# A recurrence and eight hashed experts on one core: the first decay products turned in SBUF, slot tables built by matrix products, experts with 416 places

## The chip, the core and the metric

The kernel runs on one core of a Trainium2 chip. It is one launch that computes two blocks one after the other: an RWKV-7 recurrence, and a layer of eight experts whose tokens are chosen by a hash. The metric is the device time in microseconds (us). It was measured in three runs of the kernel before, and one further execution was taken with the hardware profiler. All times below are in us unless marked ns.

## The reference, cut to what matters

```python
# block 1: B=4, H=8, S=768, D=40, float32
for t in range(S):
    y[:, :, t] = einsum('bhd,bhde->bhe', r_t, state)
    Sa = einsum('bhde,bhe->bhd', state, a_t)
    state = state * w_t[:, :, None, :] - outer(Sa, b_t) + outer(v_t, k_t)
# bridge: (B,H,S,D) -> x of shape (B*S, H*D) = (3072, 320)
# block 2: E=8 experts, F=1024
expert_idx = token_ids * 2654435761 % 8
for e in range(E):
    mask = expert_idx == e
    out[mask] = maximum(x[mask] @ w1[e], 0) @ w2[e]
```

The multiplier of the hash is 1 modulo 8, so the expert of a token is given by the low three bits of its id. For the inputs that `setup_inputs()` makes, the eight experts get 387, 359, 415, 376, 364, 403, 371 and 397 tokens.

## The kernel before, in words

**Block 1.** The sequence is cut into 12 chunks of 64 steps. A tile `u` (0 to 23) is one chunk for two of the four batches, with 128 partitions (2 batches x 64 steps). The state update inside a chunk is rewritten with running products of the decays `w`. They are formed by `decays` (L305) in six rounds. A round covers two chunks for all 32 pairs of batch and head; its 128 partitions are four half chunks of 32 steps x 32 pairs, and a partition holds 32 steps x 40 values. VectorE multiplies forwards into `pb` (L336) and backwards into `qb` (L341), joins the segments (`own` L348 and L351, `ends`, `rends` L362 to L366), and scales both arrays (L372, L379). A later step needs them the other way round, with the time step on the partition. For that, `store` (L317) writes both to DRAM as rows `p_rows` and `q_rows` (eight DMAs of 160 KB, in pieces of 40 values, which are 160 bytes), and `tile_a` loads the rows of its tile from there into `pl` and `ql` (L420, L421, by GpSimd's queue). The loads of `a`, `b`, `k`, `r` and `v` (helper `load`, L297, SyncE's queue) also move 160-byte pieces, 512 of them in each DMA.

For each tile, `tile_a` forms `at` and `z` on VectorE (L431, L435), has them transposed by TensorE (`z_ps` L449, `t_ps` L486), and multiplies them (`a_ps`). `group_i` (L498) inverts the triangular blocks of four tiles at once, in 60 small VectorE steps (L527, L534) between transposes on VectorE (L509, L542, L543). `tile_m`, `tile_s` and `tile_b` carry the state through the chunk on TensorE, eight tiles behind `tile_a`; `tile_b` ends with the product `y_ps` and writes the rows of `x` to DRAM (L697).

**Order.** Every step is entered in a list with a time in ticks (`at_tick`), one tick per tile. The list is sorted and issued in that order, so TensorE, VectorE, ScalarE and GpSimd each take their instructions in the order of the ticks. SyncE's DMA queue is not under this list; the framework's scheduler orders it. Each queue is served in order: a DMA that waits for its data holds back those behind it. The product `y_ps` of tile `u` has the tick `u + 9` (and a part of one for its place in the chunk).

**Routing.** `routing()` is a generator whose pieces are put at ticks by the loop at its end. It ranks each token within its expert (eight instructions or so at a time, all on 128 x 24 or 128 x 192 values). From the rank it makes the token's slot. Each expert has 448 slots: three full tiles of 128 and a half tile of 64. The inverse table, from slot to token, is made by 24 indirect DMAs on GpSimd's queue that write 4-byte token numbers to `slot_tokens` in DRAM (L815), and ten loads of it into `idx_all` (L823, L827).

**Block 2.** For each expert the rows of `x` are gathered by `idx_all` (L886), transposed (`xg_ps` L895) and placed as columns `xt` (128 x 3 x 448). `up` (L912, L917) makes `ht` (eight blocks of 128 features x 448 tokens, each in a PSUM bank), and VectorE and ScalarE apply the maximum. `down` (L930) multiplies 128 tokens by `w2` and scatters the rows to the output (L935). A matrix product in float32 is recorded as two MATMUL instructions. The half tiles of two experts share one output tile: two chains of products with 64 tokens each fill the lower and the upper 64 partitions of one PSUM tile, in turn.

Tokens beyond the slots of an expert, or decays outside of limits, are handled by loops that are entered only if there are any; they run no pass on these inputs.

Of the kernel before, what the change touches and what calls it, by code (L numbers as in the profile page):

```python
# [42 lines left out]
def kernel(  # L44
# [13 lines left out]
    nc = tc.nc  # L58
# [14 lines left out]
    SLOTS = 448  # L73
    TPE = SLOTS // P
    SZ = 64
    UPE = SLOTS // SZ
    NST = E * UPE
    NOV = (N - SLOTS) // SZ
    NT = NST + NOV
    assert UPE == 2 * TPE + 1  # L80
# [24 lines left out]
    WP = 4  # L105
# [21 lines left out]
    def early_weights():  # L127

        t1 = [early.tile([P, F], F32, tag=n, name=f"w1_0{n}")[:] for n in ("pk", "nb", "ub")]
        t1[2] = t1[2][:, 0:FH]  # L130
        w1s[0] = t1
# [173 lines left out]
    def decays(ri, t_w, t0, span, t_f, span_f, stores=None):  # L305
# [8 lines left out]
        def store(i, src):  # L314
            dma = nc.scalar.dma_start if ri == 0 and i == 0 else nc.sync.dma_start
            for y in range(2 * RN):
                dma(pq_dram[ri][i][y * HC:(y + 1) * HC].rearrange("t bh e -> bh t e"),  # L317
                                  src[y * BH:(y + 1) * BH].rearrange("p (t e) -> p t e", e=D))

# [24 lines left out]
        def _():  # L344
# [3 lines left out]
            nc.scalar.copy(own[:, SEG - 1], q[:, SEG - 1, 0])  # L348
# [19 lines left out]
        @then.append  # L368
        def _():

            p = segs(x["pb"])
            nc.vector.tensor_tensor(p, p, x["rends"][:].unsqueeze(2).to_broadcast([P, SEG, SL, D]), op=OP.mult)  # L372
            if stores is None:
                store(0, x["pb"])

        @then.append
        def _():
# [3 lines left out]
            nc.scalar.copy(x["qb"][:, HC * D:], x["ends"][:, SEG])  # L381
            if stores is None:
# [17 lines left out]
        for i, f in enumerate(then):  # L400
            at_tick(t_f + span_f * i / len(then), order=8)(f)
# [4 lines left out]
    def tile_a(u):  # L406
# [6 lines left out]
        def _():  # L413
# [4 lines left out]
            p_rows, q_rows = (d[rn * C:(rn + 1) * C] for d in pq_dram[ri])  # L418
            for be in range(2):
                nc.gpsimd.dma_start(pl[half(be)], of_batches(p_rows, 2 * g + be, 1))  # L420
                nc.gpsimd.dma_start(ql[half(be)], of_batches(q_rows, 2 * g, 2))  # L421
# [5 lines left out]
        @at_tick(u - 0.6)  # L427
# [10 lines left out]
        @at_tick(u, "at_t")  # L438
# [4 lines left out]
        @at_tick(u, "z")  # L443
# [9 lines left out]
        @at_tick(u, "a")  # L453
# [41 lines left out]
    def group_i(gi, t0, t1, t2):  # L495
# [4 lines left out]
        def _():  # L500
            x["u"] = ub = early.tile([P, BLK * BLK], F32, tag="ub", name="ub")[:]
# [5 lines left out]
        def _():  # L507
            x["n"] = nb = early.tile([P, BLK * BLK], F32, tag="nb", name="nb")[:]
            nc.vector.transpose(paired(nb).rearrange("p s t k -> p t s k"), paired(x["pk"]).rearrange("p t h k -> p t k h"))  # L509
# [27 lines left out]
        def _():  # L537

            ub = paired(x["u"])
            x["ug"] = ug = work.tile([P, BLK * BLK], F32, tag="ug", name="ug", bufs=1)  # L540
            x["ut"] = ut = work.tile([P, BLK * BLK], F32, tag="ut", name="ut", bufs=1)
            nc.vector.transpose(paired(ut[:]).rearrange("p g s k -> p s g k"), ub.rearrange("p s t k -> p s k t"))  # L542
            nc.vector.transpose(paired(ug[:]).rearrange("p g t k -> p t g k"), ub.rearrange("p s t k -> p t s k"))  # L543

    def tile_m(u, t0):
# [6 lines left out]
        def _():  # L552
            ut, ug = (paired(groups[gi][n][:])[:, ti * H // 2:(ti + 1) * H // 2] for n in ("ut", "ug"))
# [159 lines left out]
    decays(0, -4.0, -3.0, 0.4, -2.5, 0.3)  # L713
    decays(1, -2.9, -1.9, 0.4, -1.4, 0.3, stores=0.36)
    decays(2, -0.65, 0.42, 0.8, 1.45, 0.6, stores=3.34)
    for ri in range(3, NR):
        t0 = ri * RN * NG - 5.0
        decays(ri, t0 - 1.0, t0, 0.7, t0 + 1.0, 0.3)
# [11 lines left out]

    idx_all = route.tile([P, E * TPE + E // 2], I32)
    src_all = route.tile([P, E * TPE + E // 2], I32)
    num = route.tile([1, NT], F32)
    owner = route.tile([1, NT], F32)

    def routing():
# [6 lines left out]
        token = const.tile([P, TPP], I32)  # L743
        nc.gpsimd.iota(token[:], pattern=[[1, TPP]], base=0, channel_multiplier=TPP)
# [385 lines left out]
```

## Time and profile before

| what | us |
|---|---|
| median of three runs (lowest to highest) | 724.65 (721.87 to 730.36) |
| the profiled execution | 728.74 |
| its span, first to last instruction | 727.0 |
| first `z_ps` product (tile 0) | starts at 33.8 |
| transposes that end the first group (`ut`, L542) | start at 119.4 |
| first `y_ps` with `mr` (tile 0, tick 9) | starts at 146.9 |
| last `y_ps` with `mr` (tile 23) | starts at 443.7 |
| first `up_ps` (expert 0) | starts at 458.8 |
| last output scatter (L935) | starts at 718.5 |

The profile gives for each engine the instructions with their lines. PE is TensorE's products, PEld its weight loads, DVE is VectorE, ACT is ScalarE, POOL is GpSimd, and a q behind an engine's name is its queue of DMA issues (SPq is SyncE's). TensorE is busy in 83% of the span, VectorE in 48%, and the mean granted TensorE clock is 0.923. The 16 DMA engines move 205,669 packets, of which 186,687 have less than 512 bytes. These shares are means over very different stages, so the reading below goes by stages.

### The profile page before, as it was taken

Reading aid. Unit: us, or ns where it says so; the run is one execution under the profiler, and the core shown is the slowest. Engines: PE = TensorE matmul, PEld = TensorE weight load, DVE = VectorE, ACT = ScalarE, POOL = GpSimd, SP = SyncE. Lnnn points to the kernel's source line nnn. Section 1 sums busy time; section 2 is a strip of 40 time slices with the busy share of each in tenths; the row PEclk is TensorE's granted clock in tenths of the full one; section 3 lists DMA queues with packets and bytes.
Section 4 is the critical chain, followed back from the end, with each engine's and each line's share of the span. In section 5 each row is a group of like instructions: output and inputs, shape, how many; then the busy total and the mean of one; then the engine's idle time right before and its main releaser. Section 6 shows DMA issues by size and latency. Waiting matters only on the chain.

```text
span 727.0 us, 21410 instructions
## 1 busy us (share of the span) xinstructions
PE 600.8 (83%) x9032; PEld 449.7 (62%) x9032; DVE 352.0 (48%) x879; ACT 297.3 (41%) x689; POOL 221.9 (31%) x360
## 2 busy tenths in 40 slices
PE   0146224899979998999999993999999999999994
PEld 0135223787868887888988983465655656565652
DVE  7685556897588797579498221222020202112010
ACT  4135312676637676777766661012131313101010
POOL 0415564233325323524232222512213031212101
PEclk9976565999979999999999998799999999999998
DMA  8999968987786668785334414924262553223000
GB/s 158 163 175 152 110 75 112 147 150 130 126 176 143 113 129 145 154 160 127 60 84 90 89 39 119 262 82 129 80 207 63 145 198 138 50 94 101 27 11 20
DMA packets 205669, 86.07 MB, mean 118 GB/s; under 512 B 186687, under 2 KB 196160, under 8 KB 205569
## 3 DMA queue, kind: packets, MB, share of 16 engines
q1 hardware_dynamic: 189056, 46.29, 37.0%
q0 software_dynamic: 12160, 37.06, 19.2%
q10 hardware_dynamic: 4352, 1.31, 0.9%
q8 instruction: 72, 1.18, 0.7%
q14 instruction: 29, 0.23, 0.1%
HBM read 68.85 MB, written 16.42 MB: 117 GB/s over the span
## 4 chain that ended last, share of the span: by engine, by line
PE 45%; issue 21%; DVE 11%; DMA 9%; SPq 6%; POOL 4%; ACT 3%; POOLq 0%; DVEq 0%; ACTq 0%
PE up_ps L912 6%; PE dn_ps L930 6%; PE y_ps L278 5%; PE rc_ps L278 4%; PE s_ps L278 3%; PE r_ps L278 3%; SPq L297 3%; SPq L317 3%; DMA qb<-in_w_dram 3%; PE x_t_ps L645 3%; PE t_ps L486 2%; POOL out_dram L935 2%; PE z_ps L449 2%; DMA kb<-in_k_dram 2%; PE nc_ps L278 2%
## 5 line engine op out<-in xcount | busy, mean ns | idle before, releaser
L920 DVE TENSOR_SCALAR ht<-up_ps 128x448 f32<-128x448 f32 x32 | 20.0, 625 | 195.6 <-PE up_ps L917 129.7
L930 PE MATMUL dn_ps<-w,ht 128*128 128x320 f32 (+1 forms) x448 | 109.5, 433 | 0.0
L930 PEld LDWEIGHTS dn_ps<-w,ht 128*128 128x128 f32 (+1 forms) x448 | 72.0, 177 | 32.1 <-issue 1.3
L912 PE MATMUL up_ps<-xt,w 128*128 128x448 f32 x224 | 87.5, 544 | 0.0
L935 POOL DMA_INDIRECT out_dram<-o,idx_all x28 | 27.7, 989 | 194.9 <-ACT o L934 189.9
L697 POOL DMA_DIRECT2D x_rows<-xs x44 | 23.2, 531 | 190.4 <-DVE xs L692 101.4
L922 ACT ACTIVATE ht<-up_ps 128x448 f32<-128x448 f32 x32 | 17.4, 545 | 129.2 <-PE up_ps L917 129.2
L912 PEld LDWEIGHTS up_ps<-xt,w 128*128 128x128 f32 x224 | 41.7, 190 | 43.1 <-issue 37.9
L449 PE MATMUL z_ps<-ident,z 128*104 128x128 f32 x192 | 33.7, 333 | 41.7 <-DVE z L435 39.9
L534 DVE TENSOR_TENSOR ub<-ub,outer 128x252 f32<-128x252 f32 (+8 forms) x180 | 63.5, 353 | 4.8
L527 DVE TENSOR_TENSOR outer<-ub,nb 128x252 f32<-128x252 f32 (+8 forms) x180 | 63.3, 352 | 5.0
L934 ACT COPY o<-dn_ps 128x320 f32<-128x320 f32 x28 | 11.9, 426 | 103.3 <-PE dn_ps L930 103.3
L449 PEld LDWEIGHTS z_ps<-ident,z 128*104 128x104 f32 x192 | 26.3, 158 | 44.9 <-DVE z L435 29.0
L451 ACT COPY z_t<-z_ps 104x512 f32<-104x512 f32 x48 | 25.8, 590 | 66.0 <-PE z_ps L449 66.0
L278 PE MATMUL rc_ps<-r_t,x_t 64*128 64x64 f32 x768 | 48.9, 276 | 3.0 <-issue 1.2
L278 PEld LDWEIGHTS rc_ps<-r_t,x_t 64*128 64x128 f32 x768 | 45.4, 188 | 5.8 <-issue 2.5
L656 DVE TENSOR_TENSOR mr<-rc_ps,after 128x1024 f32<-128x1024 f32 x24 | 29.1, 1214 | 20.5 <-PE rc_ps L278 20.5
L278 PE MATMUL a_ps<-at_t,z_t 64*64 64x64 f32 x1536 | 31.5, 237 | 6.9 <-ACT at_t L487 5.2
L420 POOL DMA_DIRECT2D pl<-p_rows x48 | 25.7, 536 | 37.4 <-DMA p_rows<-pb 19.0
L278 PEld LDWEIGHTS a_ps<-at_t,z_t 64*64 64x64 f32 x1536 | 27.9, 150 | 12.3 <-ACT at_t L487 6.9
L886 POOL DMA_INDIRECT xg<-x_rows,src_all x28 | 27.0, 965 | 25.7 <-DVE selq L1027 17.4
L479 DVE TENSOR_TENSOR mk<-a_ps,after 128x512 f32<-128x512 f32 x24 | 16.5, 687 | 32.0 <-ACT no L477 32.0
(181 smaller groups left out, 1132.3 us busy)
## 6 DMA issues: line engine op xcount, KB each, us to landing
ql<-q_rows POOLq DMA_DIRECT2D x48, 160.0 KB, 4.4
w<-in_moe_w_dram SPq DMA_DIRECT2D x10, 640.0 KB, 5.0
w<-in_moe_w_dram SPq DMA_DIRECT2D x10, 512.0 KB
al<-in_a_dram SPq DMA_DIRECT2D x48, 80.0 KB, 5.0
kb<-in_b_dram SPq DMA_DIRECT2D x48, 80.0 KB, 4.1
kb<-in_k_dram SPq DMA_DIRECT2D x48, 80.0 KB, 3.6
r<-in_r_dram SPq DMA_DIRECT2D x48, 80.0 KB, 3.7
x<-in_v_dram SPq DMA_DIRECT2D x48, 80.0 KB, 4.5
```

The lines of the kernel that those rows point to most:

```text
L278: nc.tensor.matmul(out_, lhsT=lhsT, rhs=rhs, start=start, stop=stop, skip_group_check=True)
L420: nc.gpsimd.dma_start(pl[half(be)], of_batches(p_rows, 2 * g + be, 1))
L449: nc.tensor.transpose(p[0:R, be, hp * P:(hp + 1) * P], x["z"][:, be, hp, :], ident[:])
L451: nc.scalar.copy(t[0:R, be].rearrange("p h t -> p (h t)"), p[0:R, be])
L527: nc.vector.tensor_tensor(tv, paired(x["u"])[:, 0:full[1], j:j + 1, :].to_broadcast(full), paired(x["n"])[:, j // 2, j + 1:, j % 2].unsque ...
L534: nc.vector.tensor_tensor(o, o, x["t"][:, 0:n].rearrange("p (c i k) -> p c i k", c=full[1], k=2), op=OP.add)
L656: nc.vector.tensor_tensor(t[:].rearrange("p two h t -> p (two h) t"), p[:].rearrange("p two (h t) -> p (two h) t", t=C), after[:].unsqueez ...
L697: dma(x_rows[r0:r0 + C, :], xs[half(be), :])
L886: nc.gpsimd.indirect_dma_start(out=xg[0:m], out_offset=None, in_=x_rows[:], in_offset=bass.IndirectOffsetOnAxis(ap=idx, axis=0))
L912: nc.tensor.matmul(p[:], lhsT=w1[c][:, (f0 + i) * P:(f0 + i + 1) * P], rhs=xt[:, c, 0:n], start=(c == 0), stop=False)
L930: nc.tensor.matmul(p[i * m:(i + 1) * m], lhsT=ht[:, f, c0:c0 + m], rhs=w2[f // (FP // 2)][:, f % (FP // 2), :], start=(f == 0), stop=(f == ...
L935: st = nc.gpsimd.indirect_dma_start(out=out[:], out_offset=bass.IndirectOffsetOnAxis(ap=idx, axis=0), in_=o[0:m], in_offset=None, bounds_c ...
```

## The change

Four things are changed.

- **First decays.** In round 0, `pb` and `qb` are transposed by VectorE in blocks of 32 x 32 (`turned_rows`), into two SBUF tiles whose partition is the time step. `tile_a` of tiles 0 to 3 loads `pl` and `ql` from these tiles. The eight DMAs of 160-byte pieces are gone for this round; one DMA of 128 rows x 5,120 bytes writes `p` to DRAM for the later load of `py`. The two buffers share their memory with buffers of `group_i`, which become one tile each (`nu`, and `ut` with `ug`).
- **Ticks.** The last steps of rounds 1 and 2, their stores, the first step of tiles 0 to 6 and the transposes of tiles 4 to 6 get other ticks. Three small copies per round move from ScalarE to VectorE. SyncE's queue comes out in another order: the loads of `r` and `v` for the first tiles stood 8th to 12th in its list and now come behind the stores of rounds 1 and 2.
- **Tables.** The 24 scatters and the ten loads are removed. Two numbers of each token, its tile and its row within the tile, are compared with a row of counters to give one-hot rows (`at_row` 128 x 8 x 128 and `at_tile` 128 x 8 x 68, for 8 of 24 columns of tokens at a time). `at_tile` is multiplied with the token number, and the product of both over the tokens is the table. The pieces of `routing` before that go to ticks 10.4 to 21.4, these to 24.2 to 27.8. What only the loop for tokens beyond the slots needs is moved into that loop.
- **Places.** An expert has 416 slots: three tiles of 128 and a quarter tile of 32. The quarters of four experts share an output tile: they are copied to `hs`, and `down` runs four chains of 32 tokens in turn. So `w2` has five buffers in place of three, and the tables of decays to be checked come in eight parts in place of four.

```diff
-    SLOTS = 448
-    TPE = SLOTS // P
+    TPE, SH = 3, 4
+    SP = P // SH
+    SLOTS = TPE * P + SP
...
-    WP = 4
+    WP = 8
...
+        def turned_rows(src, t):
+            nc.vector.transpose(t[:, 0:BH * D].rearrange("p (bh e) -> p e bh", e=D), src.rearrange("p (t e) -> p e t", e=D))
+            return t[:, 0:BH * D]
...
-            nc.scalar.copy(own[:, SEG - 1], q[:, SEG - 1, 0])
+            nc.vector.tensor_copy(own[:, SEG - 1], q[:, SEG - 1, 0])
...
-            if stores is None:
+            if ri == 0:
+                x["p"] = turned_rows(x["pb"], early.tile([P, 2 * BLK * BLK], F32, tag="nu", name="p_rows"))
+                nc.sync.dma_start(pq_dram[ri][0].rearrange("t bh e -> t (bh e)"), x["p"])
+            elif stores is None:
                 store(0, x["pb"])
...
+            if ri == 0:
+                x["q"] = turned_rows(x["qb"][:, D:], work.tile([P, 2 * BLK * BLK], F32, tag="ut", name="q_rows", bufs=1))
+            elif stores is None:
                 store(1, x["qb"][:, D:])
...
-            p_rows, q_rows = (d[rn * C:(rn + 1) * C] for d in pq_dram[ri])
+            p_rows, q_rows = ((rounds[0][i].rearrange("t (bh e) -> t bh e", e=D) if ri == 0 else pq_dram[ri]["pq".index(i)])
+                              [rn * C:(rn + 1) * C] for i in "pq")
...
-        @at_tick(u - 0.6)
+        late = {4: 0.45, 5: 0.3, 6: 0.15}.get(u, 0.0)
+        @at_tick({0: -0.6, 1: -0.4, 2: 0.4, 3: 1.4}.get(u, u + late - (0.1 if late else 0.6)))
...
-    decays(0, -4.0, -3.0, 0.4, -2.5, 0.3)
-    decays(1, -2.9, -1.9, 0.4, -1.4, 0.3, stores=0.36)
-    decays(2, -0.65, 0.42, 0.8, 1.45, 0.6, stores=3.34)
+    decays(0, -4.0, -3.0, 0.4, -2.5)
+    decays(1, -2.9, -1.9, 0.4, (-0.55, -0.54, -0.35, -0.3, 0.2), stores=1.34)
+    decays(2, -0.65, 0.87, 0.45, (1.87, 1.9, 2.0, 2.1, 2.2), stores=3.34)
...
-        for c in range(TPP):
-            st = nc.gpsimd.indirect_dma_start(
-                out=slot_dram[:, None],
-                out_offset=bass.IndirectOffsetOnAxis(ap=key_i[:, c:c + 1], axis=0),
-                in_=token[:, c:c + 1], in_offset=None, bounds_check=NT * SZ - 1, oob_is_err=False)
...
-        for e in range(E):
-            nc.sync.dma_start(idx_all[:, e * TPE:(e + 1) * TPE],
-                              slot_dram[e * SLOTS:e * SLOTS + TPE * P].rearrange("(c p) -> p c", p=P))
...
+        for i in range(0, TPP, PC):
...
+            for at, key in ((at_row, low_i), (at_tile, key_i)):
+                nc.vector.tensor_tensor(at, col[:, 0:full[2]].unsqueeze(1).to_broadcast(full),
+                                        key[:, part].unsqueeze(2).to_broadcast(full), op=OP.is_equal)
+                yield
+            nc.vector.tensor_tensor(at_tile, at_tile, token[:, part].unsqueeze(2).to_broadcast(full), op=OP.mult)
             yield
+            p = bank([P, NW], "tok_ps")
+            for c in range(PC):
+                mm(p, at_row[:, c], at_tile[:, c], start=c == 0, stop=c == PC - 1)
...
-        t = -3.5 if i < 1 else 0.405 if i < 10 else 3.5 + 0.18 * (i - 10) if i < 11 + TPP else 9.0 + 0.3 * (i - 11 - TPP)
+        t = -3.5 if i < 1 else NU + 0.2 + 0.3 * (i - 12) if i > 11 else 9.3 + 1.1 * i
...
-            mine = (ht, w2s[e], TPE * P)
-            if e % 2:
-                down([partner_, mine], idx_all[:, shared_tile(e)], True)
-            partner_ = mine
+            if e % SH == 0:
+                sharing = []
+            hs = mwork.tile([P, FP, SP], F32, tag="hs", name="hs", bufs=SH)
+            nc.vector.tensor_copy(hs[:], ht[:, :, TPE * P:])
+            sharing.append((hs, w2s[e], 0))
+            if len(sharing) == SH:
+                down(sharing, idx_all[:, shared_tile(e)], True)
```

## The prediction

> **What bounds the kernel now.** I read the busy time by stages first, with borders at the events of the table above. The columns are the stage, its length, busy us of the engines, the granted clock, the share of the DMA engines and GB/s.
>
> ```profile
> core 0: us, PE busy (x) PEld busy (x) DVE busy (x) ACT busy (x) POOL busy (x), PEclk, DMA share, GB/s
> 16.00:66.80 50.80, 19.17 (x314) 16.50 (x314) 35.29 (x85) 13.45 (x42) 15.40 (x29) 0.82 0.97 171
> 66.80:125.00 58.20, 18.60 (x326) 16.23 (x323) 33.77 (x84) 17.30 (x39) 34.50 (x45) 0.59 0.96 101
> 125.00:146.90 21.90, 18.74 (x427) 15.82 (x425) 19.24 (x44) 13.98 (x37) 7.31 (x13) 0.87 0.95 134
> 146.90:285.10 138.20, 126.36 (x3053) 111.11 (x3052) 109.36 (x262) 91.69 (x219) 49.57 (x98) 0.94 0.76 139
> ...
> 365.70:397.00 31.30, 31.26 (x798) 28.07 (x798) 27.83 (x74) 21.01 (x49) 9.39 (x18) 1.00 0.41 84
> ...
> 458.80:718.30 259.50, 257.97 (x970) 148.21 (x970) 45.15 (x130) 44.80 (x76) 56.02 (x63) 0.99 0.35 110
> ```
>
> Until 146.9 the DMA engines are the bound: a share of 0.95, while TensorE is busy for about a third of the time. From 146.9 to 443.7 TensorE is, with VectorE close behind it (109 of 138 us, and 27.8 of 31.3). From 458.8 it is TensorE alone. The same 0.96 moves much less from 66.8 to 125 than before, and the counts of packets say so too: 33,055 in 50.8 us (650 per us) against 22,044 in 58.2 us (379 per us).
>
> The chain of waits through that slow stage shows how it reaches the compute engines: SyncE's queue waits to issue stores (L317), then loads land late.
>
> ```profile
> 74.05 2.48 SPq L317
> 76.57 3.53 SPq L317
> ...
> 86.27 8.72 DMA al<-in_a_dram
> ...
> 103.22 14.65 DMA qb<-in_w_dram
> 117.88 6.85 DMA kb<-in_k_dram
> ```
>
> What else is in flight there is told by the rows of the slot table: 24 scatters from 65.1 to 125.0, just the slow stage.
>
> ```profile
> L815 POOL DMA_INDIRECT slot_tokens<-token,key_i x24: 971/1003/1643, 65.1 to 125.0; - x24
> ...
> DMA to landing us min/median/max: 2.7/8.8/14.3
> ```
>
> **First decays.** Now `pb` is scaled by 16.2 and `qb` by 17.6, but the loads of `ql` wait for the store of `q` until 28.75, and `z` of tile 0 starts at 32.83. In the changed order VectorE scales `pb` (until 16.2), transposes it, scales `qb`, copies 40 columns and transposes `qb`. A transpose of 128x1024 takes 1,236 ns (`nb`), so one of 1,280 columns about 1.55; with 1.48 and 0.2 this gives 21.0. The loads from SBUF then follow at once; I take the 4.1 us that lay between the first issue of `ql` and `z`, so data for `z` is there at 25.1. VectorE first does the 14 products of round 1 and `own` (17.5 to 23.2 now), so `z` comes at 27.3: 5.5 us earlier. No trace shows an SBUF source; `ql`'s median of 4.4 us from DRAM is the near row, and half or twice of it moves the start by -2 to +4.
>
> Afterwards VectorE's own list decides as much as the DMAs. From `z` of tile 0 it has: `at` and `z` of tiles 1 to 3 (1.3 each), the end of round 1 (4.8), all of round 2 (5.0+0.65+4.8), four `mk` (0.7 each), which with the waits for the loads of tiles 2 and 3 brings the group's first transpose (69.6 now) to about 51. The group's steps are 60 x 0.353 = 21.2 us and 3.7 in transposes; with four `at`/`z` and three `mk` this is 32, so `ut` and `ug` end near 84 (121.8 now). From there to the first `y` the trace of before takes 25 us, in which VectorE is nearly always busy: y starts at **about 108**.
>
> The DMAs must allow that. 77,393 packets go out by 146.9. The stores of round 0 (8 x 1,024), the scatters (24 x 128), the table's start values and the loads of `r` and `v` of tile 3 go, some 13,000 in all, and 64,300 are left. About 7,000 of them are done at 18 us, and the rest at 650 per us takes 88: 106. Both ways meet, so I take 108, a gain of **39**; with VectorE waiting once more for each round, or less than thought, 20 to 50. That the loads of `r` and `v` now stand behind the stores of rounds 1 and 2 in SyncE's queue costs nothing until tile 0 needs them (tick 8, near 85): at 0.65 an issue the queue reaches them by 77 to 80. The cover is thin; without it the start slips by those few us, and this is in the range.
>
> Here a rule is to be weighed. The Trainium skill, DMA: Bandwidth & Descriptors, "Anatomy of one DMA", fits a DMA issued by GpSimd as 2.0 us plus its bytes at 436 GB/s. A scatter of 512 bytes would then cost 2 us beside the other traffic, and taking it away would give nothing on the path: the 66.8 to 125 stage would keep its 379 packets per us, and y would start near 18 + 57,300/379 = 169. The trace has 8.8 us to landing, and a rate of 552 (19,327 in 35 us, 30 to 65) to 650 before the scatters and 636 (13,930 in 21.9 us) after them. I go with the trace.
>
> **Routing pieces.** They leave the start (35.8 to 44.5 now, beside late loads) for ticks 10 to 21. About 40 instructions of 0.17 to 0.61, as in the rows there, are 8.5 us of VectorE, and two products of 192 columns 0.5 of TensorE; `past` and `owner` (3 us) go. VectorE is busy for 0.79 of that stage, TensorE for 0.91. If all is hidden it is 0, if nothing 9; I take **+4.5**. Queued behind each piece are `st` and `mr`, for which TensorE waits.
>
> **One-hot products.** Three times a comparison of 1,024 columns, one of 544, a product of 544 and an addition of 68. By `mr` (1,024 columns in 1.22) that is 1.2+0.65+0.65+0.25, so 8.3 us with the last four small ones. Some 7.2 stand before the transposes of the last group. There VectorE has this much room:
>
> ```profile
> 392.78 0.22 DVE L534 TENSOR_TENSOR ub<-ub,outer 128x60 f32<-128x60 f32 x1
> 394.32 1.22 DVE L656 TENSOR_TENSOR mr<-rc_ps,after 128x1024 f32<-128x1024 f32 x1 [1.32 <-PE rc_ps L278]
> ```
>
> It catches up with TensorE only at 393, by 1.3 us. So about 6 us show there. TensorE's 24 products of 68 columns are 48 instructions; at 0.13 each, as the transposes of 128x128 (`x_t_ps`, 8 in 1.02), they are 6.2, of which two thirds lie inside that delay and a third behind it. Together **+8**: at least 4 where TensorE's idle moments take it, 12 if the two add up. The new `tok_ps` products stand in TensorE's list before `nc_ps`, so the chain of the tile waits for the last comparison.
>
> **Between the blocks.** SyncE's queue now issues six loads of 640 KB (`w2` of experts 3 to 5, five buffers) behind the last rows of `x`, where it was two (446.7). They share the DMA engines with the first gathers (449.1 to 457.1). 2.6 MB more at the 262 GB/s of the richest slice are 10 us of DMA time; the fourth gather is what the first product waits for. **+2**, 0 to 6.
>
> **Experts.** The chain there is TensorE without a gap:
>
> ```profile
> 490.23 6.01 PE up_ps L912 x16
> 496.24 1.70 PE up_ps L917 x8
> ...
> 507.32 17.38 PE dn_ps L930 x80
> ...
> 541.66 12.92 PE dn_ps L930 x48
> ```
>
> An expert's `up` is 2 x (6.21+1.71) = 15.84. The time goes with the columns (388 ns for 448, 269 for 320), so 416 save 32/448 of it: 1.13 x 8 = **-9.0**. The shared tile of a pair is 17.38-12.92 = 4.46 for 32 instructions, 139 ns each, half of the 269 of a full one: two chains of 64 columns run side by side. Four such tiles are 17.8. The two tiles that replace them have 64 instructions each. At the pair's 139 ns they are 8.9 each, and nothing is saved. The Trainium skill, TensorEngine Tiling (Array Packing), "Theoretical Speedup", says up to 4 times for 32 columns; that makes 4.4 each and **-8.9**. I take this, since the pair has all of its factor of two, and nothing near is slower than the 67 ns it asks for: weights of 128x64 load in 38 (`r_ps`, 16 in 0.61), and 32x32 products are issued every 20 (32 of `x_ps` in 0.63). Two tiles fewer to transpose (1.46-1.13 each): **-0.7**. The copies to `hs` lie beside TensorE, with VectorE at 45 of 259 us. If there were no such cover they would cost 0.35 x 8. The largest expert has 415 tokens, so 416 places do, and the loop for the rest stays shut.
>
> **Sum.** -39+4.5+8+2-9.0-8.9-0.7 = -43.1 on the profiled execution's 728.74 (span 727.0 and 1.7 around it): 685.6. It stands 4 above the median of the runs, so in terms of that median 724.65-43.1 = **682**.
>
> **Rivals.** (1) *The start is only part shortened.* Each round still puts eight stores before the loads in SyncE's queue, and those wait for VectorE. If each of the three rounds before the first `y` holds the loads back for 9 us, the gain is 12 and not 39: -16, **708**. For it: L317 is 11% of the chain from 60 to 147. Against: after 125 such stores go out in 8 us.
> (2) *The slow packets are not the scatters' doing* but that of 160-byte stores and loads meeting, which stay. Then y starts at 169, +22; with +14.5 for the rest and -18.6 in the experts it is **742**, slower than before. It decides from 431 packets per us downwards, where y starts at 151. Against it: stores of rounds 0 and 1 and of round 3 go with loads at 552 to 650.
> (3) *Quarter tiles at the pair's pace:* **691**.
> (4) *More is gained*: with the slot loads out of SyncE's queue the ticks after the first `y` (15.3 us each up to 285, 13.4 then) tighten by 1.5 us for twelve ticks: **664**.
> (5) That 416 places don't suffice and the loop runs: excluded by the counts.
>
> **Chances.** Forecast (672 to 702) 0.60, (1) 0.20, (2) 0.05, (3) 0.07, (4) 0.08. Faster by over 1% 0.91, within 1% 0.04, slower 0.05; 1% is about what a measurement of this kernel tells from no change. The range reaches over (4) and most of (1), with the bounds of the one-hot stage: 660 to 712.
>
> **What would show it.** First `z_ps` near 28; rate of packets from 30 to 100 at 550 or more; `ut` of group 0 near 84; first `y_ps` near 108; last `y_ps` some 27 us earlier than 443.7; ticks 24 to 27 longer by 6 with VectorE without a pause; `up_ps` at 360 ns, shared tiles at 4.4. Wrong would make it loads of `r` and `v` that arrive after tick 8 has come, a rate that stays under 430, or VectorE as the bound of ticks 10 to 21.

## The result and the profile after

The changed kernel takes **675.6 us** (median of 4 runs, 672.5 to 678.2) against 726.4 us of the kernel before in the runs beside it (4 runs, 721.9 to 730.4): ratio **0.930, 95% interval 0.9225 to 0.9377**. The prediction was 682, with a range of 660 to 712. The profiled execution took 677.6 us, with a span of 675.8 after 727.0.

The total is nearly met, but not by the parts that were forecast. The events of the two traces cut the span into pieces (first `mr` is the start of L656 before and L674 after, tick 9):

| piece | before | after | difference | predicted |
|---|---|---|---|---|
| start to first `mr` | 144.9 | 114.2 | -30.7 | -39 |
| ticks 9 to 24 (16th `mr`) | 219.6 | 211.6 | -8.0 | +4.5 |
| ticks 24 to 28 | 40.2 | 46.4 | +6.2 | +8 |
| ticks 28 to 32 | 37.7 | 37.7 | 0 | 0 |
| last `mr` to first `up_ps` | 16.4 | 17.9 | +1.5 | +2 |
| first `up_ps` to last output scatter | 259.7 | 241.1 | -18.6 | -18.6 |
| after that | 8.5 | 6.8 | -1.7 | 0 |
| span | 727.0 | 675.8 | -51.2 | -43.1 |

The -39 had been forecast for the first `y_ps`, which moved by -30.3, from 146.9 to 116.6.

The busy time by stages of the changed kernel, with the columns of the prediction's first view and borders at the events after (first transpose of group 0 at 57.0, `ut` at 89.2, first `y_ps` at 116.6):

```profile
16.00:57.00 41.00, 16.64 (x310) 14.24 (x310) 33.54 (x64) 13.65 (x38) 13.93 (x27) 0.90 0.94 177
57.00:89.20 32.20, 15.61 (x256) 13.66 (x256) 28.89 (x76) 13.28 (x29) 10.50 (x21) 0.60 1.01 176
89.20:116.00 26.80, 21.31 (x474) 18.19 (x477) 24.19 (x57) 14.88 (x38) 7.25 (x14) 0.76 0.92 146
...
325.80:372.20 46.40, 45.99 (x1066) 41.34 (x1062) 38.85 (x96) 27.44 (x63) 12.50 (x24) 1.00 0.46 114
...
427.90:669.50 241.60, 239.41 (x964) 142.84 (x964) 43.22 (x128) 45.72 (x90) 54.15 (x61) 0.99 0.34 110
```

The stage in which the DMA engines moved 101 GB/s at a share of 0.96 is gone; until 89 they move 176 to 177. They are still at their limit: a share of 0.94 and 1.01. The fourth line is ticks 24 to 28: TensorE is busy for 45.99 of 46.40 us. The last one is the experts, TensorE again without a gap.

VectorE's list of the changed kernel shows what the new transposes cost and where the start comes out (start, duration, engine, line, operation, shape, and in brackets the wait before it with what ended it):

```profile
15.96 2.71 DVE L324 STREAM_TRANSPOSE p_rows<-pb 128x1280 f32<-128x1280 f32 x1
20.13 2.69 DVE L324 STREAM_TRANSPOSE q_rows<-qb 128x1280 f32<-128x1280 f32 x1
29.24 0.83 DVE L452 TENSOR_TENSOR z<-kb,ql 128x640 f32<-128x640 f32 x1 [0.29 <-DMA qb<-in_w_dram]
...
57.01 1.24 DVE L527 STREAM_TRANSPOSE nu<-pk 128x1024 f32<-128x1024 f32 x1
```

The transposes take 2.7 us each where the prediction had 1.55, and tile 0's `z` starts at 29.2 (predicted 27.3, before 32.8).

### The profile page after: what moved, and what is told of

It is laid out like the page before. It is cut to its first block, busy times and chain, and to the rows that moved or that the text cites. A ratio compares the mean times of both kernels' runs of the same rounds, so it can differ in the third digit from the quotient of the medians.

```text
span 675.8 us, 21416 instructions
## 1 busy us (share of the span) xinstructions
PE 584.4 (86%) x9074; PEld 446.2 (66%) x9074; DVE 362.0 (54%) x911; ACT 295.2 (44%) x691; POOL 194.9 (29%) x334
## 4 chain that ended last, share of the span: by engine, by line
PE 52%; issue 21%; DVE 11%; DMA 6%; POOL 4%; SPq 4%; ACT 2%; POOLq 0%; DVEq 0%; ACTq 0%
PE up_ps L934 6%; PE dn_ps L952 6%; PE y_ps L281 6%; PE rc_ps L281 5%; PE s_ps L281 4%; PE t_ps L503 3%; PE x_t_ps L663 3%; PE r_ps L281 3%; SPq L300 3%; PE a_ps L281 3%; DMA qb<-in_w_dram 3%; POOL out_dram L957 2%; PE sd_ps L723 2%; PE x_ps L281 2%; PE u_ps L281 2%
## 5 line engine op out<-in xcount | busy, mean ns | idle before, releaser
L942 DVE TENSOR_SCALAR ht<-up_ps 128x416 f32<-128x416 f32 x32 | 18.9, 592 | 179.3 <-PE up_ps L939 177.6
L952 PE MATMUL dn_ps<-w,ht 128*128 128x320 f32 x336 | 91.7, 433 | 0.0
L934 PE MATMUL up_ps<-xt,w 128*128 128x416 f32 x224 | 81.3, 516 | 0.0
L952 PEld LDWEIGHTS dn_ps<-w,ht 128*128 128x128 f32 x336 | 63.3, 190 | 25.5
L957 POOL DMA_INDIRECT out_dram<-o,idx_all x26 | 26.1, 1002 | 177.9 <-ACT o L956 173.0
L944 ACT ACTIVATE ht<-up_ps 128x416 f32<-128x416 f32 x32 | 16.5, 517 | 122.4 <-PE up_ps L939 122.3
L934 PEld LDWEIGHTS up_ps<-xt,w 128*128 128x128 f32 x224 | 41.9, 190 | 36.9 <-issue 31.7
L552 DVE TENSOR_TENSOR nu<-nu,outer 128x252 f32<-128x252 f32 (+8 forms) x180 | 63.4, 352 | 4.7
L545 DVE TENSOR_TENSOR outer<-nu 128x252 f32<-128x252 f32 (+8 forms) x180 | 63.4, 352 | 4.7
L466 PE MATMUL z_ps<-ident,z 128*104 128x128 f32 x192 | 31.9, 320 | 16.3 <-DVE z L452 14.6
L674 DVE TENSOR_TENSOR mr<-rc_ps,after 128x1024 f32<-128x1024 f32 x24 | 29.1, 1214 | 17.9 <-PE rc_ps L281 17.9
L908 POOL DMA_INDIRECT xg<-x_rows,src_all x26 | 25.2, 969 | 25.2 <-DVE selq L1054 17.6
```

Of the source, the lines that this page charges most:

```text
L466: nc.tensor.transpose(p[0:R, be, hp * P:(hp + 1) * P], x["z"][:, be, hp, :], ident[:])
L545: nc.vector.tensor_tensor(tv, paired(x["u"])[:, 0:full[1], j:j + 1, :].to_broadcast(full), paired(x["n"])[:, j // 2, j + 1:, j % 2].unsque ...
L552: nc.vector.tensor_tensor(o, o, x["t"][:, 0:n].rearrange("p (c i k) -> p c i k", c=full[1], k=2), op=OP.add)
L674: nc.vector.tensor_tensor(t[:].rearrange("p two h t -> p (two h) t"), p[:].rearrange("p two (h t) -> p (two h) t", t=C), after[:].unsqueez ...
L908: nc.gpsimd.indirect_dma_start(out=xg[0:m], out_offset=None, in_=x_rows[:], in_offset=bass.IndirectOffsetOnAxis(ap=idx, axis=0))
L934: nc.tensor.matmul(p[:], lhsT=w1[c][:, (f0 + i) * P:(f0 + i + 1) * P], rhs=xt[:, c, 0:n], start=(c == 0), stop=False)
```

## Experiments: the start

**The scatters alone.** The kernel before, with the last of the routing pieces and the scatters at ticks 22 to 26 in place of 0.4 to 8, and the reading of the table after them.

```diff
-        t = -3.5 if i < 1 else 0.405 if i < 10 else 3.5 + 0.18 * (i - 10) if i < 11 + TPP else 9.0 + 0.3 * (i - 11 - TPP)
+        t = -3.5 if i < 1 else 0.405 if i < 9 else 22.0 + 0.18 * (i - 10) if i < 11 + TPP else 26.6 + 0.22 * (i - 11 - TPP)
```

> The kernel before with one thing moved: the start values of the slot table, its 24 scatters, the ten loads of it and what is computed from them go from ticks 3.3 to 13 to ticks 21.8 to 29.4. Theory S (the scatters slow every packet of the start): 73,900 packets at 650 per us after the first 8,400 by 16 us put the first mr near 117 (144.9 before), and the ticks 9 to 24 lose the two VectorE stalls of 8.9 us, with 0 to 5 us coming back in ticks 24 to 29; total near 690. Theory T (the turned decays and the new order of the queue make the gain of the start): the first mr stays at 138 or later and the total at 712 to 726.

Measured: 726.1 us in the median, ratio 0.992 (0.9877 to 0.9967), and not the 690 of theory S. The trace is of the shortest of ten executions (718.4). Its first `mr` came at 124.9, **20.0 us earlier**; in the four traced kernels that keep the 4-byte writes in the start it lies between 143.9 and 151.7. Much was given back where the scatters now stand: ticks 24 to 28 took 52.3 for 40.2, and ticks 9 to 24 only 1.1 us less than before. The stage that had held the scatters, in the kernel before and then in this one:

```profile
67.00:120.00 53.00, 15.91 (x256) 13.76 (x255) 29.43 (x75) 15.37 (x34) 32.17 (x42) 0.60 0.97 94
```

```profile
67.00:120.00 53.00, 30.16 (x591) 25.51 (x593) 45.97 (x112) 25.43 (x63) 16.25 (x32) 0.61 0.85 147
```

It moves 147 GB/s instead of 94, and 28,874 packets instead of 18,956 (545 per us instead of 358). The slow packets were the scatters' doing. Rival (2) falls with this, and so does the price of 2 us for a DMA of 512 bytes, as far as what it does to others is concerned.

**Are they slow because they are indirect?** The kernel before, with each scatter replaced by a plain DMA of the same 128 x 4 bytes to consecutive places. The table is then in the order of the tokens and not of the slots, so the routing is left out of the result.

```diff
-            st = nc.gpsimd.indirect_dma_start(
-                out=slot_dram[:, None],
...
+            nc.gpsimd.dma_start(slot_dram[c * P:(c + 1) * P].unsqueeze(1), token[:, c:c + 1])
```

> The kernel before with each scatter replaced by a plain DMA on the same queue at the same place, of the same 128 pieces of 4 bytes, to 128 neighbouring words; the table is then in the order of the tokens, so rows of the output are computed with wrong experts and some are left out. If 4-byte writes to DRAM as such slow the rest: the rate from 67 to 125 stays under 450 packets per us and the first mr at 140 or later. If the place ahead of pl and ql on GpSimd's queue does it: first mr late too, but with idle DMA engines (share under 0.85). If the indirect form does it: 550 packets per us or more and the first mr at 117 to 125.

Measured in a single run: 731.6 us, first `mr` at 151.7, and the same stage as slow as before:

```profile
67.00:120.00 53.00, 14.70 (x245) 12.75 (x244) 24.92 (x61) 13.73 (x31) 18.37 (x36) 0.53 1.10 92
```

So the indirect form is not the cause. Nor is GpSimd's work for it (18.4 us of POOL here for 32.2), nor the place in GpSimd's queue, which should have left the DMA engines idle: their share is 1.10. What holds the others up is 24 DMAs of 128 pieces of 4 bytes to DRAM. They are 12 KB in all and cost about 20 us. The profile counts 32 packets for each of them: up to the first `y`, GpSimd's queue has 2,656 packets before and 1,888 after, with the same 48 loads. So 768 of 77,393 packets are enough. Whether it is the size of the pieces, their number, or that all go to one small table was not varied.

**The turned decays alone.** The changed kernel with round 0's decays stored to DRAM in 160-byte pieces as before, the four stores of `p` on ScalarE's queue.

```diff
+            dma = nc.scalar.dma_start if ri == 0 and i == 0 else nc.sync.dma_start
...
-            if ri == 0:
-                x["p"] = turned_rows(x["pb"], early.tile([P, 2 * BLK * BLK], F32, tag="nu", name="p_rows"))
-                nc.sync.dma_start(pq_dram[ri][0].rearrange("t bh e -> t (bh e)"), x["p"])
-            elif stores is None:
+            if stores is None:
```

> The kernel after with round 0 sent through DRAM as before (eight stores of 160-byte pieces, loads from there); everything else as in the kernel after. Theory S: 8,064 packets more at 602 per us are 13 us at most, and first z returns to 33 from 29.2; the first mr comes at 119 to 128 (114.2 after), total 681 to 690. Theory T: the first mr is back at 138 or later, total 699 or more.

Measured: 680.3 us, ratio 0.934 (0.9294 to 0.9393; the changed kernel 0.930). Tile 0's `z` came at 28.9, no later than with the transposes, and the first `mr` at 116.1, 1.9 us later than at 114.2 and earlier than the text had expected. The turning is worth about **2 us**, at the edge of what the runs can tell. The stores of `q` in SyncE's queue, before and in this run, and `z` of tile 0 in this run:

```profile
23.40 3.40 SPq L317 DMA_DIRECT2D q_rows<-qb  x4
```

```profile
17.58 5.32 SPq L320 DMA_DIRECT2D q_rows<-qb  x4
...
28.93 0.83 DVE L447 TENSOR_TENSOR z<-kb,ql 128x640 f32<-128x640 f32 x1 [1.93 <-DMA ql<-q_rows]
```

`z` comes early in both kernels, for different reasons. In this run the stores no longer stand behind the loads of `r` and `v`, and `z` waits for `ql`. In the changed kernel VectorE works almost without a pause up to `z`, which waits 0.29 us, and 5.4 us of that work are the two transposes. They take about as long as the way through DRAM did.

From 124.9 (scatters moved) to 116.1 (all of the change but the turning) 8.8 us are left. The next two runs look for them.

**Routing pieces back in the start.** The changed kernel with its first eleven routing pieces at tick 0.405.

```diff
-        t = -3.5 if i < 1 else NU + 0.2 + 0.3 * (i - 12) if i > 11 else 9.3 + 1.1 * i
+        t = -3.5 if i < 1 else NU + 0.2 + 0.3 * (i - 12) if i > 11 else 0.405
```

> The changed kernel with the eleven first routing pieces back at tick 0.405, where they stood before. Theory (of the 9 us by which the first mr comes earlier than with the scatters alone moved, most is the VectorE time of these pieces): first mr near 121, 6 to 8 us later than in the changed kernel, ticks 9 to 24 shorter by 0 to 2, the whole longer by 5 to 8. Rival (the pieces lie beside VectorE's waits for loads in the start, and the new ticks and queue order gave the 9): first mr at 114 to 116, and the whole the same within 2 us.

Measured: 686.1 us, ratio 0.943 (0.9388 to 0.9467). First `mr` at 124.0, **9.8 us later**, the first transpose of group 0 at 69.2 instead of 57.0; ticks 9 to 24 shorter by 2.1. Theory and rival had asked for 6 to 8 us and for none. The pieces do not lie beside waits: they cost the start more than their own 8.5 us, and ticks 9 to 24 only 2.1.

**Old ticks.** The changed kernel with the former ticks of rounds 1 and 2 and of tiles 0 to 6.

```diff
-        late = {4: 0.45, 5: 0.3, 6: 0.15}.get(u, 0.0)
+        late = 0.0
...
-        @at_tick({0: -0.6, 1: -0.4, 2: 0.4, 3: 1.4}.get(u, u + late - (0.1 if late else 0.6)))
+        @at_tick(u - 0.6)
...
-    decays(1, -2.9, -1.9, 0.4, (-0.55, -0.54, -0.35, -0.3, 0.2), stores=1.34)
-    decays(2, -0.65, 0.87, 0.45, (1.87, 1.9, 2.0, 2.1, 2.2), stores=3.34)
+    decays(1, -2.9, -1.9, 0.4, -1.4, stores=0.36)
+    decays(2, -0.65, 0.42, 0.8, (1.45, 1.57, 1.69, 1.81, 1.93), stores=3.34)
```

> The changed kernel with the ticks that the decays of rounds 1 and 2 and the first tiles had before. Theory (routing pieces gave the 9 us): first mr at 113 to 117. Rival (ticks and the order of SyncE's queue gave them): first mr at 119 to 124, and the whole longer by 5 to 9. Together with the run that puts the routing pieces back the two should make about 9; if both show little, each covers for the other.

Measured: 685.9 us, between 681.7 and 692.2, ratio 0.9445 (0.9374 to 0.9516). First `mr` at 121.4, 7.2 later; ticks 9 to 24 shorter by 3.4. The two runs together make 17 us and not the 9 that were looked for. So the parts of the start don't add up: each of them, taken out alone, costs about as much as the whole 8.8. A likely reason is that whatever fills VectorE's list or holds the loads before 57 moves all that follows; no run shows it. Of these 17 us, 5.5 come back in ticks 9 to 24.

**What holds the start now?** In the changed kernel tile 2's `z_ps` waits for 3.8 us on TensorE behind `f_ps` of round 2. First that half of round 2 was put behind tile 2's steps.

```diff
-    decays(2, -0.65, 0.87, 0.45, (1.87, 1.9, 2.0, 2.1, 2.2), stores=3.34)
+    decays(2, -0.65, 0.87, 0.45, (2.87, 2.88, 2.9, 2.95, 3.0), stores=3.34)
```

> The changed kernel with the second half of round 2's decays (f_ps to en_ps) behind tile 2's z, transposes and first products in the lists of TensorE, ScalarE and VectorE, where it stands ahead of them; SyncE's and GpSimd's lists are the same. Theory (after the scatters are gone, what holds the first group is that order: tile 2's z_ps waits 3.8 us behind f_ps): group 0's first transpose comes at 52 to 54 instead of 57.0, and the first mr at 110 to 112 instead of 114.2. Rival (the DMA engines, with a share of 0.94 to 1.01 at 177 GB/s until 89, hold it): the first transpose comes earlier, the first mr not by more than 1 us.

Measured: 675.5 us, ratio 0.937 (0.9322 to 0.9413). First transpose at 56.5 (0.5 us earlier), first `mr` at 113.2 (1.0 earlier). By the letter these are the rival's numbers, but TensorE's list shows that the order was not mended: tile 3's `z_ps` now stood behind `en_ps`, which waited for `ends`:

```profile
45.52 0.42 PE L363 MATMUL f_ps<-own,partner 128*128 128x40 f32 x2
48.52 0.40 PE L401 MATMUL en_ps<-ident,ends 128*40 128x128 f32 x1 [2.59 <-DVE ends L370]
48.72 1.91 PE L466 MATMUL z_ps<-ident,z 128*104 128x128 f32 x8
```

The wait was handed on, not removed, so this run decides nothing. In a second one (with half floats as below, which touch only later ticks) `en_ps` stands behind tile 3 as well.

```diff
-    decays(2, -0.65, 0.87, 0.45, (2.87, 2.88, 2.9, 2.95, 3.0), stores=3.34)
+    decays(2, -0.65, 0.87, 0.45, (2.87, 2.88, 2.9, 2.95, 3.9), stores=3.34)
```

> The kernel with half floats and round 2 behind tile 2, with one step more: en_ps and its copies stand behind tile 3's z, transposes and products too. In the run before, the wait was only handed on: tile 3's z_ps stood behind en_ps, which waited for ends until 48.5, and the first transpose came at 55.6 to 56.5. Theory (that order holds the start): now tile 3's z_ps starts near 46, the first transpose at 52 to 54, and the first mr at 109.5 to 111.5, the whole 2 to 4 us less, 669 to 671. Rival (the DMA engines, or VectorE's list with them, hold it further on): the first transpose at 52 to 54, but the first mr at 113 or later, and the whole within 1 us of 672.8.

Measured: 675.8 us, ratio 0.9315 (0.9275 to 0.9356). VectorE's list of this run:

```profile
53.36 1.23 DVE L528 STREAM_TRANSPOSE nu<-pk 128x1024 f32<-128x1024 f32 x1
58.95 0.82 DVE L453 TENSOR_TENSOR z<-kb,ql 128x640 f32<-128x640 f32 x1 [1.48 <-DMA kb<-in_k_dram]
...
83.82 0.82 DVE L453 TENSOR_TENSOR z<-kb,ql 128x640 f32<-128x640 f32 x1 [2.83 <-DMA kb<-in_k_dram]
...
89.04 1.24 DVE L561 STREAM_TRANSPOSE ut<-nu 128x1024 f32<-128x1024 f32 x1
```

The first transpose comes 3.6 us earlier than in the changed kernel, but `ut` still at 89.0 (89.2 there) and the first `mr` at 113.7. What was gained is spent on waits of `z` for the loads of `kb` (1.48 and 2.83), which the changed kernel does not have there. From 57 to 89 the DMA engines have a share of 1.05 in this run. So the loads hold the start up to 89, not the order of round 2. How far this is the issue order of SyncE's queue (those for the last of these `z` start at 75.5) and how far the engines' own limit was not told apart.

## Experiments: the ticks after the start

**Where do 8 us of ticks 9 to 24 come from?** In the trace of before, VectorE stands still twice in ticks 11 to 13:

```profile
188.51 0.18 DVE L832 TENSOR_SCALAR src_all<-idx_all 128x28 int32<-128x28 int32 x1 [5.32 <-DMA x<-in_v_dram]
...
201.49 0.58 DVE L843 CAST ends_f<-ends_i 1x8 f32<-1x8 int32 x1 [3.60 <-POOL ends_i L841]
```

The first waits for the ten loads of the table (the DMA named is one that stands beside them in the queue), the second for GpSimd. Both instructions are in VectorE's list ahead of the tiles' work. To test this, the kernel before with only the reading of the table at ticks 26.6 and later:

```diff
-        t = -3.5 if i < 1 else 0.405 if i < 10 else 3.5 + 0.18 * (i - 10) if i < 11 + TPP else 9.0 + 0.3 * (i - 11 - TPP)
+        t = -3.5 if i < 1 else 0.405 if i < 10 else 3.5 + 0.18 * (i - 10) if i < 10 + TPP else 26.6 + 0.22 * (i - 10 - TPP)
```

> The kernel before with only the reading of the slot table (ten loads, the clamp of it, owner) moved to ticks 26.6 to 29.4; the scatters stay at ticks 3.5 to 7.8. If the two VectorE stalls (src_all 5.3 us, ends_f 3.6 us) are what the kernel after saves between tick 9 and tick 24, then mr 9 to mr 24 of the list shortens by about 8 (219.6 to 211) with the first mr unchanged near 145: total near 718. If they were hidden, that stretch stays within 2 us of 219.6 and the total near 726.

Measured: 723.8 us in the median, ratio 0.993 (0.989 to 0.997). In the trace (an execution of 731.3 us) ticks 9 to 24 took 219.5 us, as long as before. That is what the text had expected of hidden waits, but the place tells more. Both waits lie between the third and the fifth `mr`, here before and after the change:

```profile
172.52 1.22 DVE L656 TENSOR_TENSOR mr<-rc_ps,after 128x1024 f32<-128x1024 f32 x1
...
211.02 1.22 DVE L656 TENSOR_TENSOR mr<-rc_ps,after 128x1024 f32<-128x1024 f32 x1
```

```profile
143.04 1.22 DVE L674 TENSOR_TENSOR mr<-rc_ps,after 128x1024 f32<-128x1024 f32 x1
...
173.46 1.22 DVE L674 TENSOR_TENSOR mr<-rc_ps,after 128x1024 f32<-128x1024 f32 x1
```

| kernel | the two waits | third to fifth `mr` | rest of ticks 9 to 24 |
|---|---|---|---|
| before | there | 38.5 | 181.1 |
| plain writes | there | 38.7 | 176.6 |
| experts' part alone (below) | there | 39.0 | 175.0 |
| this run | moved | 29.9 | 189.6 |
| scatters late | moved | 29.9 | 188.5 |
| the changed kernel | gone | 30.4 | 181.2 |

With the waits the stretch takes 38.5 to 39.0 us, without them 29.9 to 30.4. So the two waits are not hidden, and **all of the -8.0** of the changed kernel lies where they stood. What this run gained there it lost later: from the 14th to the 15th `mr` it takes 6.4 us more. There TensorE pauses for 3.2 us, for which the profile names no cause, and then has a granted clock of 0.61 for 7.9 us. Whether the loads of the table, which SyncE's queue now issues at that place, have to do with it was not tested.

**The one-hot products: TensorE or VectorE?** The list of TensorE in the changed kernel, one of three groups:

```profile
336.18 2.00 PE L281 MATMUL tok_ps<-at_tile,at_row 128*128 128x68 f32 x16
338.11 0.68 PE L281 MATMUL nc_ps<-r,um 64*64 64x40 f32 x32
```

Starts lie 1.93 us apart, three groups are 5.8 us: nearly all of the +6.2, if no part of it is hidden. First the twelve steps were moved to later ticks, where VectorE has less to do.

```diff
-        t = -3.5 if i < 1 else NU + 0.2 + 0.3 * (i - 12) if i > 11 else 9.3 + 1.1 * i
+        t = -3.5 if i < 1 else NU + 3.15 + 0.25 * (i - 12) if i > 11 else 9.3 + 1.1 * i
...
-    at_tick(NU + 4.0)(early_weights)
+    at_tick(NU + 6.5)(early_weights)
```

> The changed kernel with the one-hot products' twelve steps moved from ticks 24 to 26.5 to ticks 27.15 to 29, and the early weights to 2.5 ticks later. Theory (the 6.2 us that ticks 24 to 28 took more are TensorE's own: three groups of 16 products at 1.93 us, which no place hides): ticks 24 to 28 fall by 4 to 6 us, ticks 28 to 32 grow by as much, and the whole stays within 2 us. Rival, as in the prediction (VectorE's 7 us ahead of the last transposes show there): away from those transposes the comparisons lie beside other work, the two stretches together shorten by 3 to 6 us, and the whole by as much, ratio 0.925.

Measured: 677.7 us, ratio 0.929 (0.9252 to 0.9335). Ticks 24 to 28 took 41.9 (-4.5) and ticks 28 to 32 41.4 (+3.7). The stages of both, in this run:

```profile
327.41:369.29 41.88, 41.80 (x1034) 37.61 (x1028) 33.86 (x84) 27.49 (x63) 12.55 (x24) 1.00 0.45 97
369.29:410.72 41.43, 39.41 (x922) 36.04 (x924) 13.83 (x24) 22.21 (x51) 7.33 (x14) 1.00 0.28 70
```

One of the three groups still stands in the first stage (1,034 products against 1,018 before) and two in the second. That stage grew by 3.7 us, two times 1.93, though VectorE has work for only 13.8 of its 41.4 us. That is TensorE's own time, and the 3 to 6 us of the rival did not come. Then the same products in one pass: one-hot rows in 16-bit floats, and the tokens as -1536 to 1536 without zero, which such floats hold exactly.

```diff
-            at_row = early.tile([P, (HC + 1) * D], F32, tag="qb", name="at_row", bufs=2)[:, 0:PC * P].rearrange("p (c x) -> p c x", c=PC)
+            at_row = early.tile([P, (HC + 1) * D], F32, tag="qb", name="at_row", bufs=2)[:, 0:PC * P // 2].bitcast(F16).rearrange("p (c x) -> p c x", c=PC)
...
-        token = route.tile([P, TPP], F32)
-        nc.vector.tensor_copy(token[:], token_i[:])
+        token = route.tile([P, TPP], F16)
+        nc.vector.tensor_scalar(token[:], token_i[:], float(-N // 2), None, op0=OP.add)
...
+        nc.vector.scalar_tensor_tensor(tokens[:], tokens[:], 0.0, tokens[:], op0=OP.is_le, op1=OP.add)
```

> The changed kernel with the one-hot rows, and the tokens counted from -1536 to 1536, in 16-bit floats, so that a product of the three groups takes one pass where it takes two. Theory (the stage of the one-hot products is longer by TensorE's own time for them): a group's products fall from 1.93 us to 0.5 to 1, ticks 24 to 28 from 46.4 to 42 to 44, the whole by 3 to 4 us, ratio near 0.925. Rival (VectorE's comparisons, which stay, hold the stage): ticks 24 to 28 stay at 45 to 46.5 and the whole within 1 us.

Measured: 674.1 us, ratio 0.932 (0.928 to 0.9366). One group of its products, the longest wait of TensorE that came up, and ticks 24 to 28, whose line for the changed kernel is the fourth of the stages above:

```profile
335.29 0.43 PE L282 MATMUL tok_ps<-at_tile,at_row 128*128 128x68 f16 x8
...
348.96 1.13 PE L282 MATMUL y_ps<-z,mr 128*64 128x40 f32 x32 [1.35 <-DVE mr L675]
```

```profile
324.94:369.38 44.44, 42.05 (x1042) 36.93 (x1036) 38.73 (x97) 27.49 (x63) 12.53 (x24) 1.00 0.46 117
```

TensorE loses 4.0 us of work, the stretch only 2.0, and TensorE now has 2.4 us without work, most of it waiting for VectorE. So the truth lies between the two: TensorE's time showed first, and right behind it stands VectorE's. They cover each other and don't add up.

Both small improvements together:

> The half floats and round 2 behind tile 2, both in the changed kernel. If the two are independent, its time is the changed kernel's less the sum of their gains: 5 to 8 us, 668 to 671, ratio near 0.921. If the start is held by the DMA engines, 3 to 4 us, and if VectorE holds the one-hot stage, nothing.

Measured: 672.8 us, ratio 0.932 (0.9281 to 0.9352). Against the changed kernel's 0.930 (0.9225 to 0.9377) none of the variants is measurably faster; in their traces they are 3 to 4 us shorter at most (span 672.1 for 675.8). Half floats at the later ticks, where VectorE is far from its limit, would be the next thing to try; that was not run.

## Experiments: the experts

The kernel before with nothing of the change but 416 places and shared tiles of four.

```diff
-    SLOTS = 448
-    TPE = SLOTS // P
+    TPE, SH = 3, 4
+    SP = P // SH
+    SLOTS = TPE * P + SP
...
+    PITCH = UPE * SZ
...
-        t = wpool.tile([P, FP, DM], F32, tag="w2", name=f"w2_{e}", bufs=3)
+        t = wpool.tile([P, FP, DM], F32, tag="w2", name=f"w2_{e}", bufs=5)
```

> The kernel before with nothing of the change but the 416 places and the shared tiles of four (tables with room for 448 places per expert, w2 with five buffers). Theory (four chains of 32 columns run side by side): the experts, from the first up to the last output scatter, shorten from 259.7 to 241 us, and the whole by 17 to 19: ratio near 0.975, about 708. Rival (a quarter tile costs at the pair's pace, and something else of the change shortened the experts): only the 9 to 10 of up are saved, ratio near 0.987. The rest of the kernel keeps its times: first mr at 145 within 2, ticks 9 to 24 in 219 to 220, 24 to 28 in 40.

Measured: 708.8 us, ratio 0.974 (0.9697 to 0.9778). From the first `up_ps` to the last output scatter 242.0 us instead of 259.7. A shared tile of four here, and then in the changed kernel:

```profile
690.98 4.51 PE L933 MATMUL dn_ps<-w,hs 128*32 128x320 f32 x64
```

```profile
663.68 4.51 PE L952 MATMUL dn_ps<-w,hs 128*32 128x320 f32 x64
```

64 instructions in 4.51 us, where the pair's tile took 4.46 for 32. At the pair's pace they would be 8.9, so rival (3) falls. The way from the last `mr` to the first `up_ps` is 18.5 us here against 16.4, so some 2 us come with the experts' part. That the six loads of `w2` are their cause is argued; no run took them out alone. One thing stays open: ticks 9 to 24 were 5.6 us shorter than before in this trace, though both waits of VectorE are still in it (6.13 and 3.61 us). The gain lies outside of the waits, as the table above shows. TensorE did the same 5,089 products in 202.8 us there for 205.7, at a granted clock of 0.98 for 0.95, which is about half of it. The medians of the runs, 18.4 us apart, leave no room for it beside the experts' gain, so it may be no more than one execution's.

## Why the prediction was right, and where it was not

**The range and the sign** hold, and the forecast is 6.4 us above the measured median. Two steps missed by about 8 and 12 us, on opposite sides, so that they mostly cancel in the sum. That the total came so near is luck.

**Start: -39 forecast, -30.7 measured.** The mechanism was right: the scatters slowed all other DMA traffic. The price of one DMA by itself (the Trainium skill, DMA: Bandwidth & Descriptors, "Anatomy of one DMA"), from which the prediction had worked out a first `y` near 169, leaves out what a DMA does to the others; `y` came at 116.6. Three things in the working were off.
- The currency. 64,300 packets at 650 per us gave 106. Measured are 67,528 packets up to 117.6, and 602 per us from 16 on. A scatter was counted as 128 packets, and the profile has 32, so some 2,300 fewer went than was thought. The mean packet grew from 262 bytes in the stage with 650 per us to 284 in the changed kernel. Bytes fit better: that stage moved 171 GB/s, and the changed kernel moves 16.7 MB from 16 to 114.2, which is 170.
- The transposes: 2.7 us each for 1.55, scaled from the group's, which reads in steps of 8 bytes where this one reads in steps of 160. This makes 2.3 us, and `z` came 1.9 late.
- From `z` of tile 0 to the group's first transpose 27.8 us instead of 23.7: TensorE's list, where tile 2's `z_ps` waits behind `f_ps`, was not followed. In the run with round 2 last it is 24.0, but the loads then come too late for a gain. The other 2.6 us lie between that transpose and the first `y` (59.6 for 57) and were not looked into.

The shares of the start were also wrong. The headline item, the turned decays, is worth 2 us; the scatters alone gave 20, and the rest comes with the ticks and with the routing pieces, whose leaving was given no gain of its own in the prediction.

**Ticks 9 to 24: +4.5 forecast, -8.0 measured.** This is the step that failed. The cost of the pieces was within its bounds (2.1 us by the run that puts them back, of 0 to 9). Missed were two waits of VectorE, 8.9 us by its list: one for the loads of the table, one for GpSimd. Both went with the reading of the table, and the stretch that held them is 8.1 us shorter. The prediction counted `past` and `owner` as 3 us of work that goes, and the wait ahead of `ends_f` right before them not at all. Rival (4) had the direction, and the loads of the table as the cause. But it spread 18 us beyond the forecast over twelve ticks, where 12.5 came, and the gain lies in ticks 11 to 13 alone.

**Ticks 24 to 28: +8 forecast, +6.2 measured.** The number of instructions was right, and TensorE's price was 0.12 each for 0.13. The prediction let VectorE's delay show first (6) and a third of TensorE's time behind it; in fact the two overlap, and TensorE's is the greater. Its sign, VectorE without a pause, did not come: VectorE is busy for 38.9 of 46.4 us, TensorE for 46.0.

**Between the blocks** +1.5 for +2; that it is the six loads is argued. **Experts** -18.6 for -18.6, and -17.7 in the run with this part alone: `up` by its columns, and the factor of 4 for 32 columns (the Trainium skill, TensorEngine Tiling (Array Packing), "Theoretical Speedup", with which this trace agrees: 4.51 us for 64 instructions are 70 ns each, for 139 at the pair and 269 at a full tile). The last 1.7 us, after the last scatter, were not in the sum, and no run looked at them.

**Rivals.** (1) would have needed 9 us for each round of stores; round 0, put back with half of its stores on ScalarE's queue, cost 2. Rounds 1 and 2 were not taken out. (2) needed 431 packets per us or less: with the scatters moved, the stage has 545. (3) is excluded by the shared tile, and (4) half right as said.

## What to carry to other kernels

Look for the smallest writes in a stage whose DMA share is high but whose GB/s are low: here 3,072 writes of 4 bytes cost 20 us, in which the same engines move 3.4 MB at 171 GB/s. Moving them shifted much of the cost and did not remove it (12 of the 20 us came back in ticks 24 to 28). Count a DMA-bound stage in bytes as well as in packets, since packets per us depend on which of them are left. For every operation that is removed, read the wait in front of it too: here two waits ahead of instructions of 0.2 and 0.6 us were worth 8 us, and all that the change added in those ticks cost 2.

## What the hardware showed that was not expected

- While 24 DMAs of 128 x 4 bytes to DRAM are queued, plain or indirect alike, the 16 DMA engines stay at 92 to 94 GB/s and 350 to 358 packets per us; with the scatters moved away the same stage has 147 GB/s and 545 packets per us.
- A 32 x 32 block transpose on VectorE took 2.7 us for 128 x 1,280 values that it reads and writes in steps of 160 bytes on both sides, and 1.24 us for 128 x 1,024 in the group's transposes, which read in steps of 8 bytes and write pairs of neighbours: 2.1 ns for a column against 1.2. No run varied the steps alone.
- Products of a 128 x 128 one-hot tile with 68 columns start 121 ns apart in float32 (16 for a group of 8), and the same 8 products in 16-bit floats take 0.43 us instead of 1.93.
